# Matmul operands of odd width made even in an attention and long-convolution kernel

## The chip, the cores and the metric

The kernel runs on one core of a Trainium2 chip. The metric is device time in microseconds, the median of several executions. Before the change it is 371.0 us (three runs: 370.59, 371.0 and 372.24 us).

In the profile PE is TensorE (matmuls), PEld is TensorE loading the stationary operand, DVE is VectorE, ACT is ScalarE, POOL is GpSimd and SP is SyncE, which issues most transfers. "L905" is line 905 of the kernel. A matmul has a stationary operand (up to 128 columns, loaded ahead) and a moving operand, which is streamed through; "128\*128 128x65" is a matmul with 128 rows and 128 columns of weights and a moving operand of 65 columns.

## The reference

Softmax attention with an extra 1 in the denominator, and behind it a gated long convolution along the sequence, done by a real Fourier transform. The shapes: batch 8, 12 heads, sequence S = 448, head width 64, so the model width D is 768.

```python
scores = scale * np.matmul(q, k.transpose(0, 1, 3, 2))
m = np.max(scores, axis=-1, keepdims=True)
e = np.exp(scores - m)
attn = e / (np.sum(e, axis=-1, keepdims=True) + np.exp(-m) + 1e-09)
x = np.matmul(attn, v)                         # then [batch, S, 768]
proj = x @ w_proj                              # three parts of 768: x1, x2, x3
X2 = np.fft.rfft(x2, n=S, axis=1)
H = np.fft.rfft(filter_fft, n=S, axis=0)[None, :, :]
x2_conv = np.fft.irfft(X2 * H, n=S, axis=1)
out = (x1 * x2_conv * x3) @ w_out
```

Inputs and output are 32-bit floats; the kernel computes its matmuls in bfloat16 and sums in 32 bits.

## The kernel before

The kernel has 48 attention steps (8 batches by 6 pairs of heads, `attention(i)`) and 8 dense steps (one for each batch, `dense(b)`), woven into one another. Every piece of work is a task given to a planner by `add(...)`, with its engine, an estimate of its cost, what it needs and what it makes. The order in which the tasks are issued on each engine is written out by hand, a long list of numbers in `plan.ORDER`, one for each `add` in the order of the calls. The planner goes through it in a small model of the chip only to assign the eight banks of PSUM (each 512 columns of 32 bits); the order on an engine does not depend on the costs. So each engine runs one fixed sequence, and waits for semaphores where its next instruction needs another engine's result.

An attention step: `scores` multiplies the transposed keys kT and queries qT, 64 rows for each head of the pair (L866, moving operand of 448 columns) and one matmul of 128 rows for the last 64 keys of both heads (L868). `exps` writes the exponentials e and er to SBUF (ACT, L879 and L885). Then the exponentials are the stationary operand and the values the moving one: `out_rests` (L897) makes 4 by 2 matmuls of 64 rows for the last keys, the two heads one after the other on the upper and lower 64 rows, and `out_rest` (L905) makes 12 of 128 rows for each head. The value tiles vn hold 64 value columns and a column of ones for each head, so a matmul also gives the sum of the exponentials: their width is DH + 1 = 65 columns, and a pair of PSUM banks takes 2 heads by 4 blocks by 65 columns (`out_banks`). `norm` (DVE: L918, L919, L920) divides by that sum plus one, and frees the banks. GpSimd casts the values from 32 bits into vn (L531, L695, and L551, L649 for the last keys) and sets the ones once for each of the two vn buffers (`ones`, L1506).

A dense step for batch b: the real Fourier transform is made of four tables (pg = 0 to 3: cosine and sine, even and odd frequencies) on a folded sequence. `first` and `second` (DVE, L1045 and L1050) fold x to four parts of FQ = 113 columns. The folded tile xf is laid out as [4 parts, 6 blocks of D, 114], of which 113 columns are used, so the four parts of one block are not next to each other. In batches 0 to 2 xf is the stationary operand of the projection (`proj2`, L1073). In batches 3 to 7 it is the moving one (`still2`, L1095): four runs of 113 columns, 452 in all, written to a PSUM bank as 452 columns next to each other, six matmuls for each of six blocks, 180 in all. `still2_back` copies the bank to SBUF (DVE L1106, ACT L1108). Then come the spectrum (L1144, L1148), its product with the filter's (DVE), and the inverse transform: `inverse` (L1243) makes four matmuls for each of six blocks, 192 in all, with the inverse table bt as the moving operand, 113 columns, and writes them to 4 by 113 columns of a bank; `inverse_back` (ACT, L1252) copies these to cr. DVE unfolds cr and multiplies by the gates x1 and x3, which are projections of x as well (`gate`, L1196, 448 columns, 576 matmuls). `output` (L1009, 384 columns) is the last projection, and `project_back` (ACT, L1318) and a transfer write it out.

The table bt is made once in `more_tables` (`turn_back`, L788 and L791).

Of the kernel before, what the change touches and what calls it, by code (L numbers as in the profile page):

```python
# [15 lines left out]
BF16 = mybir.dt.bfloat16  # L16
I32 = mybir.dt.int32

B, H, S, DH = 8, 12, 448, 64
D = H * DH  # L20
SP = 112
NST = S // SP
NDT = D // 128
NHP = H // 2
SCALE = 1.0 / float(np.sqrt(DH))
DCH = 384
HALF = S // 2
FQ = SP + 1
# [286 lines left out]
def kernel(  # L315
# [11 lines left out]
    nc = tc.nc  # L327
# [6 lines left out]
    WHOLE = (5, 6, 7)  # L334
# [22 lines left out]
    const = ctx.enter_context(tc.tile_pool(name="const", bufs=1))  # L357
    wts = ctx.enter_context(tc.tile_pool(name="wts", bufs=1))
# [4 lines left out]
    fold = ctx.enter_context(tc.tile_pool(name="fold", bufs=1))  # L363
# [5 lines left out]

    ft = wts.tile([FQ, 4, FQ], BF16, name="ft")  # L370
    fr = hyp.tile([FQ, 4, FQ], BF16, name="fr", tag="yR")
    bt = wts.tile([FQ, 4, FQ], BF16, name="bt")
    wproj_bf = wts.tile([128, NDT, 3 * D], BF16, name="wproj_bf")
    wout_bf = wts.tile([128, NDT, D], BF16, name="wout_bf")

# [18 lines left out]

    kT = [const.tile([128, NHP, 4, 128], BF16, name=f"kT{i}") for i in range(2)]
    qT = [const.tile([128, NHP, S], BF16, name=f"qT{i}") for i in range(2)]
    vn = [const.tile([128, NHP, 7, DH + 1], BF16, name=f"vn{i}") for i in range(2)]
    ks_flat = const.tile([128, NHP * 128], BF16, name="ks")
    ks = ks_flat.rearrange("p (g c) -> p g c", g=NHP)

# [10 lines left out]
    x2s = nat[:, 0:KNAT].rearrange("p (t a n) -> p t a n", t=NDT, a=4)  # L411
# [33 lines left out]
    def bank(hy):  # L445
        i = plan.banks[hy][0]
        return psum[:, 512 * i : 512 * i + 512]
# [5 lines left out]
    def pair(hy):  # L453
        i = plan.banks[hy][0]
        return psum[:, 512 * i : 512 * i + 1024].rearrange("p (u n) -> p u n", u=2)
# [310 lines left out]
    def more_tables():  # L766
        bb = lambda: bank2(("hy", "bps"))[:, 0 : 4 * (FQ + 1)].rearrange("p (a b) -> p a b", a=4)

        def mirror():
            rps = bank(("hy", "rps"))  # L770
            nc.tensor.matmul(
                rps[:FQ, 0 : 4 * FQ], tab["jm"][:FQ, :], ft[:].rearrange("p a b -> p (a b)")
            )

        def mirror_back():

            rps = bank(("hy", "rps"))
            nc.vector.tensor_copy(fr[:].rearrange("p a b -> p (a b)"), rps[:FQ, 0 : 4 * FQ])
            nc.vector.tensor_scalar(
                fr[:, 1:3, :].rearrange("p a b -> p (a b)"), rps[:FQ, FQ : 3 * FQ], -1.0, None, op0=ALU.mult  # L780
            )

        def turn():
            for pg in range(4):
                nc.tensor.transpose(bb()[:FQ, pg, 0:FQ], tab["sb"][:FQ, pg, 0:FQ], ident_bf[:FQ, :FQ])

        def turn_back():
            nc.vector.tensor_scalar(  # L788
                bt[:, 0, 0:FQ], bb()[:FQ, 0, 0:FQ], tab["half"][:FQ, 0:1], None, op0=ALU.mult
            )  # L790
            nc.vector.tensor_copy(bt[:, 1:4, 0:FQ], bb()[:FQ, 1:4, 0:FQ])  # L791

        add("POOL", 1.1, WT, weights, need=["row"], make=["half"], after=WT)
        add("DVE", 0.25, FT, after=FT, emit=lambda: nc.vector.tensor_scalar(
            ft[:], tab["sb"][:FQ, :, 0:FQ], tab["half"][:FQ, 0:1], None, op0=ALU.mult), need=["sines", "half"],
            make=["ft"])
        add("PE", 0.25, 29.0, mirror, need=["ft", "half"], make=["rps"], take=[("hy", "rps")], after=29.0)
        add("DVE", 0.95, 25.0, mirror_back, need=["rps"], make=["fr"], take=[("yR", "fr")], give=[("hy", "rps")])
        add("PE", 0.25, BPS, turn, need=["ident", "sines"], make=["bps"], take=[("hy", "bps")], after=BPS)
        add("DVE", 0.45, BPS, turn_back, need=["bps", "half"], make=["bt"], give=[("hy", "bps")])  # L800

    W = {}
# [51 lines left out]
    def attention(i):  # L854
        b, hp = divmod(i, NHP)
        P = T.setdefault(i, {})
# [28 lines left out]
                nc.scalar.activation(to, of, AF.Exp, scale=SCALE)  # L885

        def out_banks():
            return pair(("op", i))[:, :, 0 : NST * (DH + 1)].rearrange("p u (n d) -> p u n d", n=NST)

        def out_bank(u):  # L890
            return out_banks()[:, u]
# [125 lines left out]
    def dense(b, calm=True):  # L1017

        L = {}
# [8 lines left out]
        def mem(name, make):  # L1028
            if (name, b) not in W:
                W[name, b] = make()  # L1030
            return W[name, b]
# [13 lines left out]
            nc.vector.tensor_tensor(t[:, 0 : ds.stop - ds.start], lo, hi, op=(ALU.add, ALU.subtract)[n])  # L1045

        def second(ds, pg):
            xf = mem("xf", lambda: fold.tile([128, 4, NDT, FQ + 1], BF16, name="xf"))
            t = L["uuww"[pg], ds.start][:, 0 : ds.stop - ds.start]
            nc.vector.tensor_tensor(  # L1050
                xf[:, pg, ds, 0:FQ],
                t[:, :, 0:FQ],
                t[:, :, HALF : HALF - FQ : -1],
                op=(ALU.add, ALU.subtract, ALU.subtract, ALU.add)[pg],
            )

# [13 lines left out]
        def proj2(pg, ch, hy):  # L1070
            L["P", pg, ch] = pps = bank(hy)
            for kt in range(NDT):
                nc.tensor.matmul(  # L1073
                    pps[:FQ, :DCH],
                    W["xf", b][:, pg, kt, 0:FQ],
                    wproj_bf[:, kt, D + ch * DCH : D + (ch + 1) * DCH],
                    start=(kt == 0),
                    stop=(kt == NDT - 1),
                )
# [10 lines left out]
            return mem("x2", lambda: hyp.tile([128, NDT, 4, 128], BF16, name="x2", tag="x2"))  # L1090

        def still2(dt, hy):
            L["P", dt] = pps = bank(hy)[:, 0 : 4 * FQ].rearrange("p (a n) -> p a n", a=4)
            for kt in range(NDT):
                nc.tensor.matmul(  # L1095
                    pps,
                    wproj_bf[:, kt, D + dt * 128 : D + (dt + 1) * 128],
                    W["xf", b][:, :, kt, 0:FQ],
                    start=(kt == 0),
                    stop=(kt == NDT - 1),  # L1100
                )

        def still2_back(dt):
            to, of = (x2s if b in WHOLE else W["xb", b])[:, dt, :, 0:FQ], L["P", dt]
            if dt % 2:
                nc.vector.tensor_copy(to, of)  # L1106
            else:
                nc.scalar.copy(to, of)  # L1108
# [128 lines left out]
        PLACE = (0, 1, 3, 2)  # L1237

        def inverse(dt, hy):
            L["I", dt] = cps = bank(hy)  # L1240
            for pg in range(4):
                K, par, rs = BLK_K[pg], pg // 2, pg % 2
                nc.tensor.matmul(  # L1243
                    cps[:, PLACE[pg] * FQ : (PLACE[pg] + 1) * FQ],
                    W["yh", b][:K, par, rs, dt * 128 : (dt + 1) * 128],
                    bt[:K, pg, :],
                )

        def inverse_back(dt):
            if ("cr", dt // 2) not in L:  # L1250
                L["cr", dt // 2] = small.tile([128, 2, 4, FQ], BF16, name="cr")
            nc.scalar.copy(  # L1252
                L["cr", dt // 2][:, dt % 2].rearrange("p a n -> p (a n)"), L["I", dt][:, 0 : 4 * FQ]
            )

        def halves(dp, n):
# [203 lines left out]
    with (  # L1460
# [42 lines left out]
        add("POOL", 0.8, 7.0, pads, make=["pads"], after=6.5)  # L1503

        def ones(i):
            nc.gpsimd.memset(vn[i][:, :, :, DH : DH + 1], 1.0)  # L1506
        for i in range(2):
            add("POOL", 0.08, (6.0, 24.0)[i], lambda i=i: ones(i), make=[("ones", i)],
                after=(6.5, 16.0)[i])
# [81 lines left out]
```

## Time and profile before

| what | value |
|---|---|
| median of the runs | 371.0 us |
| lowest and highest run | 370.59, 372.24 us |
| span of the profiled execution, first to last instruction | 369.2 us |
| mean granted TensorE clock in the span | 0.999 |
| transfers, mean rate | 185 GB/s, 68.41 MB |
| chain of work that ended last | L1009 1.4%, L1318 0.1% of the span |

The span is one execution under the profiler. That execution's own time outside its span isn't in the profile; the median of the three runs stands 1.8 us above the span.

The busy times of the engines say how full each is. A matmul's record is longer than the time until the next one starts, because matmuls overlap in the array; so what a matmul costs TensorE is read from the distance of starts, in the timeline, and not from the mean duration of its group. In a row of the timeline the first number is the start in us from the span's start, the second the time that the group spans, and "x24" how many instructions were put together. In a row of groups stand the count, then the busy time in us, the mean duration in ns, and the idle time before them with what ended it. In a row of waits stand the total in us, how often, and the longest.

### The profile page before, as it was taken

The page shows a single profiled execution, that of the slowest core. Times are in us where ns is not written, and L with a number is a line of the kernel's source. Part 1 is how long each engine was busy: PE and PEld are TensorE (multiplying, and loading weights), DVE is VectorE, ACT ScalarE, POOL GpSimd, SP SyncE. Part 2 cuts the span into 40 slices and gives each one's busy share as a digit, 9 for nine tenths or more (in the row PEclk, how much of TensorE's full clock was granted, in tenths as well). Part 3 has the DMA queues.
Part 4 walks back from the last instruction along what each step waited for, and adds up shares of the span by engine and source line. Part 5 has one row for each costly group of instructions (what it writes and reads, how often), then busy time and mean ns, then how long its engine had stood idle before and what let it go on. Part 6 is the DMA issues. An engine that isn't in the chain of part 4 may idle for free. (4 is left out here: it accounts for less than half of the span.)

```text
span 369.2 us, 9353 instructions
## 1 busy us (share of the span) xinstructions
PE 361.6 (98%) x3613; PEld 217.1 (59%) x3613; DVE 258.3 (70%) x671; ACT 263.0 (71%) x453; POOL 112.6 (30%) x247
## 2 busy tenths in 40 slices
PE   8999999999999999999999999999999999999995
PEld 6766665656664675654555555665556556555653
DVE  5569388967699648883796868773577845968570
ACT  6889686787777778687688468877778586545623
POOL 7862732344524455414125430411300000000000
PEclk9999999999999999999999999999999999999999
DMA  8999999797998999689999999799855064243125
GB/s 207 273 242 227 255 228 228 174 203 198 183 274 211 221 271 251 181 196 215 259 222 249 229 218 175 224 239 180 197 113 124 2 88 130 42 103 71 43 91 172
DMA packets 132019, 68.41 MB, mean 185 GB/s; under 512 B 88765, under 2 KB 128384, under 8 KB 131968
## 3 DMA queue, kind: packets, MB, share of 16 engines
q1 hardware_dynamic: 127248, 62.11, 74.0%
q0 software_dynamic: 4480, 5.41, 8.4%
q8 instruction: 29, 0.48, 0.6%
q10 hardware_dynamic: 240, 0.23, 0.3%
q14 instruction: 22, 0.18, 0.2%
HBM read 43.86 MB, written 11.01 MB: 149 GB/s over the span
## 5 line engine op out<-in xcount | busy, mean ns | idle before, releaser
L879 ACT ACTIVATE e<-psum 128x896 bf16<-128x896 f32 x138 | 122.2, 922 | 29.9 <-PE psum L866 27.9
L1196 PE MATMUL psum<-xT,wproj_bf 128*128 128x448 bf16 x576 | 121.2, 352 | 0.0
L1196 PEld LDWEIGHTS <-wproj_bf 128*128 128x128 bf16 x576 | 53.9, 98 | 45.6 <-issue 2.2
L1009 PE MATMUL psum<-wout_bf,yT 128*128 128x384 bf16 x288 | 53.1, 326 | 0.0
L663 POOL CAST nat<-nat 112x512 bf16<-112x512 f32 x36 | 23.7, 664 | 88.0 <-DMA nat<-in_q_dram 77.6
L905 PEld LDWEIGHTS <-e 128*128 128x128 bf16 x1104 | 40.5, 98 | 9.8 <-issue 5.8
L905 PE MATMUL psum<-vn,e 128*128 128x65 bf16 x1104 | 46.2, 194 | 0.0
L866 PE MATMUL psum<-qT,kT 64*128 64x448 bf16 x288 | 43.6, 358 | 2.1 <-DVE xb L920 1.4
L1162 DVE TENSOR_TENSOR t<-xs,hrs 113x768 bf16<-113x768 bf16 (+1 forms) x64 | 35.8, 588 | 7.2 <-ACT xs L1156 7.1
L1156 ACT CAST xs<-psum 112x384 bf16<-112x384 f32 (+1 forms) x64 | 29.2, 484 | 15.5 <-PE psum L1144 10.9
L1009 PEld LDWEIGHTS <-yT 128*128 128x128 bf16 x288 | 27.1, 98 | 18.7 <-issue 1.1
L1095 PE MATMUL psum<-xf,wproj_bf 128*128 128x452 bf16 x180 | 38.1, 356 | 0.0
L1318 ACT COPY osb<-psum 128x384 f32<-128x384 f32 x56 | 26.1, 485 | 14.6 <-PE psum L1009 9.3
L920 DVE TENSOR_TENSOR xb<-psum,den 128x512 bf16<-128x512 f32 x48 | 33.2, 691 | 1.7
L1212 DVE TENSOR_TENSOR g<-x,psum 128x448 bf16<-128x448 bf16 x42 | 25.9, 617 | 10.0 <-PE psum L1196 8.0
L885 ACT ACTIVATE er<-psum 128x448 bf16<-128x448 f32 x46 | 25.5, 554 | 8.1 <-PE psum L868 7.9
L1210 ACT CAST x<-psum 128x448 bf16<-128x448 f32 x42 | 22.4, 540 | 10.5 <-PE psum L1196 8.4
L1252 ACT CAST cr<-psum 128x452 bf16<-128x452 f32 x48 | 24.1, 551 | 6.3 <-PE psum L1243 6.3
L918 DVE TENSOR_SCALAR den<-psum 128x8 f32<-128x8 f32 x48 | 7.9, 164 | 28.3 <-PE psum L905 21.5
L695 POOL CAST vn<-nat 128x192 bf16<-128x192 f32 x58 | 23.1, 427 | 14.5 <-DMA nat<-in_v_dram 14.3
L1095 PEld LDWEIGHTS <-wproj_bf 128*128 128x128 bf16 x180 | 16.4, 96 | 17.1 <-issue 1.7
L1073 PE MATMUL psum<-wproj_bf,xf 128*113 128x384 bf16 x144 | 26.4, 327 | 0.0
(136 smaller groups left out, 484.7 us busy)
## 6 DMA issues: line engine op xcount, KB each, us to landing
nat<-in_q_dram SPq DMA_DIRECT2D x47, 224.0 KB, 4.3
out_dram<-osb SPq DMA_DIRECT2D x24, 384.0 KB, 3.8
nat<-in_k_dram SPq DMA_DIRECT2D x41, 192.0 KB, 4.6
nat<-in_v_dram SPq DMA_DIRECT2D x41, 192.0 KB, 4.4
wproj_bf<-in_moe_w_proj_dram POOLq DMA_DIRECT2D x2, 1152.0 KB, 12.3
rests<-in_k_dram SPq DMA_DIRECT2D x8, 192.0 KB, 4.8
rests<-in_v_dram SPq DMA_DIRECT2D x8, 192.0 KB, 3.9
out_dram<-osb SPq DMA_DIRECT2D x8, 192.0 KB, 3.9
```

Of the source, the lines that this page charges most:

```text
L866: nc.tensor.matmul(sc[:, u, 0:S], kT[b % 2][c, hp, t, :], qT[b % 2][c, hp, :])
L879: nc.scalar.activation(to, of, AF.Exp, scale=SCALE)
L905: nc.tensor.matmul(out_bank(u)[:, n, :], P["e"][1 + t][:, u * S + n * 128 : u * S + n * 128 + 128], vn[b % 2][:, hp, 4 * u + t, :], start= ...
L920: nc.vector.tensor_tensor(W["xb", b][:, hp].rearrange("p n (u d) -> p u n d", u=2), op[:, :, :, 0:DH], rec[:].unsqueeze(3).to_broadcast([1 ...
L1009: nc.tensor.matmul(ops[:n, :DCH], y[:, dt, 0:n], wout_bf[:, dt, ch * DCH : (ch + 1) * DCH], start=(dt == 0), stop=(dt == NDT - 1),)
L1073: nc.tensor.matmul(pps[:FQ, :DCH], W["xf", b][:, pg, kt, 0:FQ], wproj_bf[:, kt, D + ch * DCH : D + (ch + 1) * DCH], start=(kt == 0), stop= ...
L1095: nc.tensor.matmul(pps, wproj_bf[:, kt, D + dt * 128 : D + (dt + 1) * 128], W["xf", b][:, :, kt, 0:FQ], start=(kt == 0), stop=(kt == NDT - 1),
L1156: nc.scalar.copy(L["xs", par, ch][:K, pg % 2, :], L["Z", pg, ch][:K, :DCH])
L1162: nc.vector.tensor_tensor(t[:K], L["xs", par, ch][:K], h, op=ALU.mult)
L1196: nc.tensor.matmul(p[:, :S], wproj_bf[:, kt, 2 * part * D + dt * 128 : 2 * part * D + (dt + 1) * 128], xT()[:, kt, 0:S], start=(kt == 0), ...
L1212: nc.vector.tensor_tensor(g[:, dt, :], L["x1", dt], p[:, :S], op=ALU.mult)
L1318: nc.scalar.copy(L["os", st][:n, ch * DCH : (ch + 1) * DCH], L["O", st, ch][:n, :DCH])
```

## The change

Three moving operands get an even width. The value tiles vn have 66 columns for each head in place of 65; the second of the two ones columns gives a second copy of the sum, which nobody reads. The folded x is laid out as [6 blocks, 4 parts, 114], so that the four parts of a block are one run of 456 columns; the 114th column of each part is a sum or difference that nobody reads, and `second` writes it too. The inverse table bt has 114 columns for each part, the last one zero (a memset). The tiles in PSUM grow with them, and the copies out of PSUM skip the columns that were added. No task is added or taken away, and neither the order of the tasks nor their costs in the planner change.

```diff
-    bt = wts.tile([FQ, 4, FQ], BF16, name="bt")
+    bt = wts.tile([FQ, 4, FQ + 1], BF16, name="bt")
...
-    vn = [const.tile([128, NHP, 7, DH + 1], BF16, name=f"vn{i}") for i in range(2)]
+    vn = [const.tile([128, NHP, 7, DH + 2], BF16, name=f"vn{i}") for i in range(2)]
...
             nc.vector.tensor_copy(bt[:, 1:4, 0:FQ], bb()[:FQ, 1:4, 0:FQ])
+            nc.vector.memset(bt[:, :, FQ:], 0.0)
...
         def out_banks():
-            return pair(("op", i))[:, :, 0 : NST * (DH + 1)].rearrange("p u (n d) -> p u n d", n=NST)
+            return pair(("op", i))[:, :, 0 : NST * (DH + 2)].rearrange("p u (n d) -> p u n d", n=NST)
...
         def second(ds, pg):
-            xf = mem("xf", lambda: fold.tile([128, 4, NDT, FQ + 1], BF16, name="xf"))
+            xf = mem("xf", lambda: fold.tile([128, NDT, 4, FQ + 1], BF16, name="xf"))
             t = L["uuww"[pg], ds.start][:, 0 : ds.stop - ds.start]
             nc.vector.tensor_tensor(
-                xf[:, pg, ds, 0:FQ],
-                t[:, :, 0:FQ],
-                t[:, :, HALF : HALF - FQ : -1],
+                xf[:, ds, pg, :],
+                t[:, :, 0 : FQ + 1],
+                t[:, :, HALF : HALF - FQ - 1 : -1],
                 op=(ALU.add, ALU.subtract, ALU.subtract, ALU.add)[pg],
             )
...
-                    W["xf", b][:, pg, kt, 0:FQ],
+                    W["xf", b][:, kt, pg, 0:FQ],
                     wproj_bf[:, kt, D + ch * DCH : D + (ch + 1) * DCH],
...
         def still2(dt, hy):
-            L["P", dt] = pps = bank(hy)[:, 0 : 4 * FQ].rearrange("p (a n) -> p a n", a=4)
+            L["P", dt] = pps = bank(hy)[:, 0 : 4 * FQ + 4].rearrange("p (a n) -> p a n", a=4)
...
-                    W["xf", b][:, :, kt, 0:FQ],
+                    W["xf", b][:, kt],
...
         def still2_back(dt):
-            to, of = (x2s if b in WHOLE else W["xb", b])[:, dt, :, 0:FQ], L["P", dt]
+            to, of = (x2s if b in WHOLE else W["xb", b])[:, dt, :, 0:FQ], L["P", dt][:, :, 0:FQ]
...
-                    cps[:, PLACE[pg] * FQ : (PLACE[pg] + 1) * FQ],
+                    cps[:, PLACE[pg] * (FQ + 1) : (PLACE[pg] + 1) * (FQ + 1)],
                     W["yh", b][:K, par, rs, dt * 128 : (dt + 1) * 128],
                     bt[:K, pg, :],
...
             nc.scalar.copy(
-                L["cr", dt // 2][:, dt % 2].rearrange("p a n -> p (a n)"), L["I", dt][:, 0 : 4 * FQ]
+                L["cr", dt // 2][:, dt % 2], L["I", dt][:, 0 : 4 * FQ + 4].rearrange("p (a n) -> p a n", a=4)[:, :, 0:FQ]
             )
...
         def ones(i):
-            nc.gpsimd.memset(vn[i][:, :, :, DH : DH + 1], 1.0)
+            nc.gpsimd.memset(vn[i][:, :, :, DH : DH + 2], 1.0)
```

## The prediction

> **What bounds the kernel now.** I read the page's busy times first, then the waits of TensorE, then the groups by line and shape, and last the timeline, for the distance from one matmul's start to the next. The page and the waits:
>
> ```profile
> span 369.2 us, 9353 instructions
> PE 361.6 (98%) x3613; PEld 217.1 (59%) x3613; DVE 258.3 (70%) x671; ACT 263.0 (71%) x453; POOL 112.6 (30%) x247
> ...
> PEclk9999999999999999999999999999999999999999
> ...
> PE psum L866 <- DVE xb L920: 1.4, 3, 0.6
> PE psum L1487 <- DVE idle L1475: 1.1, 1, 1.1
> PE psum L866 <- DVE kT L578: 0.7, 1, 0.7
> ...
> ACT e L879 <- PE psum L866: 27.9, 37, 2.0
> DVE den L918 <- PE psum L905: 21.5, 23, 2.3
> ```
>
> TensorE is busy 98% of the span at full granted clock, and its visible waits come to 3.2 us. The two largest engines beside it wait for it (ACT 27.9 us in one group, DVE 21.5 us in another), not it for them. So the time is the sum of the matmuls' distances in TensorE's one order, and a shorter distance is worth its count. The mean durations in the groups below do not show this distance, since a matmul's record overlaps the next one's: L905 has 1104 records of 194 ns in 46.2 us. The counts are what I take from these rows:
>
> ```profile
> L1196 PE MATMUL psum<-xT,wproj_bf 128*128 128x448 bf16 x576 | 121.2, 352 | 0.0
> L905 PE MATMUL psum<-vn,e 128*128 128x65 bf16 x1104 | 46.2, 194 | 0.0
> L1095 PE MATMUL psum<-xf,wproj_bf 128*128 128x452 bf16 x180 | 38.1, 356 | 0.0
> L897 PE MATMUL psum<-vn,er 64*128 64x65 bf16 x368 | 13.5, 191 | 0.0
> L1243 PE MATMUL psum<-bt,yh 113*128 113x113 bf16 x96 | 11.9, 214 | 0.0
> L1243 PE MATMUL psum<-bt,yh 112*128 112x113 bf16 x96 | 11.8, 214 | 0.0
> L905 PE MATMUL psum<-vn,wout_bf 128*128 128x65 bf16 x48 | 1.9, 194 | 0.0
> L897 PE MATMUL psum<-vn,wout_bf 64*128 64x65 bf16 x16 | 0.6, 193 | 0.0
> ```
>
> The distances come from pairs of neighbouring groups in the timeline of TensorE: the start of the next group less the start of this one, over this one's count.
>
> ```profile
> 352.27 4.70 PE L1196 MATMUL psum<-xT,wproj_bf 128*128 128x448 bf16 x24
> 356.81 0.49 PE L1009 MATMUL psum<-wout_bf,yT 128*128 128x384 bf16 x2
> ...
> 186.32 1.14 PE L1009 MATMUL psum<-wout_bf,yT 128*128 128x384 bf16 x6
> 187.29 0.33 PE L1144 MATMUL psum<-x,ft 113*112 113x384 bf16 x1
> ...
> 22.86 0.38 PE L981 MATMUL psum<-ident_bf,xb 128*128 128x128 bf16 x4
> 23.08 0.36 PE L771 MATMUL psum<-ft,jm 113*113 113x452 bf16 x1
> ...
> 150.55 0.92 PE L905 MATMUL psum<-vn,e 128*128 128x65 bf16 x24
> 151.31 0.37 PE L1243 MATMUL psum<-bt,yh 113*128 113x113 bf16 x4
> ...
> 107.83 0.79 PE L1243 MATMUL psum<-bt,yh 113*128 113x113 bf16 x12
> 108.46 0.35 PE L1196 MATMUL psum<-xT,wproj_bf 128*128 128x448 bf16 x1
> ...
> 205.38 3.67 PE L1095 MATMUL psum<-xf,wproj_bf 128*128 128x452 bf16 x18
> 208.90 0.91 PE L905 MATMUL psum<-vn,e 128*128 128x65 bf16 x24
> ```
>
> Widths that the change leaves alone: 448 columns take 4.54/24 = 189.2 ns, 384 take 0.97/6 = 162 ns, 128 take 0.22/4 = 55 ns. They lie on one line: (189.2 - 55)/320 = 0.42 ns a column and some 2.5 ns for each matmul. Widths that it changes: 65 columns take 0.76/24 = 31.7 ns, 113 take 0.63/12 = 52.5 ns, four runs of 113 (452 in all) take 3.52/18 = 195.5 ns. The line gives 29.6, 49.6 and 190.8 ns for these. Each of the three shapes whose runs are odd lies above the line, by 2.1, 2.9 and 4.7 ns. No shape of even runs does.
>
> The Trainium skill, page "TensorE: Matmul & The Clock Gate", section "Wait — 56ns, not 53.3ns?", says that a warm matmul follows the last after N columns at 2.4 GHz plus about 2.5 ns, whatever N's parity. By it the change can only cost, for it adds columns. The trace agrees at 448 columns (189.2 ns) and contradicts it at 113 (52.5 against 49.6 ns).
>
> **The change part by part.** I take the excess to be the price of an odd run, so that the new widths fall on the line: 66 columns 30.0 ns, 114 columns 50.0 ns, 456 columns 192.5 ns.
>
> - Value tiles of 66, L905: 1104 + 48 = 1152 matmuls by 31.7 - 30.0 = 1.7 ns is 1.96 us. Bounds: 1152 by 0.4 ns more, or 0.5 us lost, if the excess stays and the column is paid on top; and 1.96 us won.
> - The same tiles in L897: 368 + 16 = 384 matmuls of 64 rows, issued as 192 pairs on the two halves of the array. The trace gives no clean distance for a pair, so between nothing and 192 by 1.7 ns = 0.33 us; I take 0.15 us, the middle.
> - Inverse tables of 114, L1243: 192 by 52.5 - 50.0 = 2.5 ns is 0.48 us. Bounds: 192 by 0.4 = 0.1 us lost to 0.48 us won.
> - Folded x as one run of 456, L1095: 180 by 195.5 - 192.5 = 3.0 ns is 0.54 us. This term needs the least: whether the excess is from odd runs or from the three breaks between runs, both are gone. Bounds: 180 by 1.7 ns = 0.3 us lost to 0.54 us won.
>
> The sum is 1.96 + 0.15 + 0.48 + 0.54 = 3.1 us of TensorE's order.
>
> The rest of the diff lies on other engines:
>
> ```profile
> L920 DVE TENSOR_TENSOR xb<-psum,den 128x512 bf16<-128x512 f32 x48 | 33.2, 691 | 1.7
> L1252 ACT CAST cr<-psum 128x452 bf16<-128x452 f32 x48 | 24.1, 551 | 6.3 <-PE psum L1243 6.3
> L1050 DVE TENSOR_TENSOR xf<-u 128x339 bf16<-128x339 bf16 x30 | 11.4, 389 | 0.1
> L1050 DVE TENSOR_TENSOR xf<-w 128x339 bf16<-128x339 bf16 x30 | 11.3, 386 | 0.3
> L1085 DVE CAST x<-psum 113x384 bf16<-113x384 f32 x12 | 6.5, 554 | 4.9 <-PE psum L1073 4.6
> L1506 POOL MEMSET vn<- 128x42 bf16 x2 | 0.5, 344 | 0.0
> L1390 DVE MEMSET low<- 128x48 f32 x1 | 0.1, 98 | 0.0
> ```
>
> The copies out of PSUM (L1252, L1106, L1108) keep their 452 elements and read them in rows of 113 at a pitch of 114. L920 already reads rows of 64 at a pitch of 65, and its 512 elements cost 691 - 554 = 137 ns over L1085's 384, or 1.07 ns an element, with nothing left for breaks. So nothing, with ACT's 551 ns hidden under TensorE as it is now. The folds (L1050) write 342 in place of 339 elements: a few ns by 64, below 0.2 us of DVE. Were the engine to take them element by element, as it does L920's, they would cost 342 by 1.07 ns and 691 - 512 by 1.07 = 143 ns, 509 ns in all, or 120 ns more by 64 = 7.7 us of DVE, a rise from 70% to 72%: still under TensorE, but up to 1 us later for the first projection of a batch, where other matmuls stand ahead of it in the order. The new memset on DVE is one of some 100 ns, in the set-up, before L1243's first use. The ones (L1506, twice) go from 42 to 84 elements: 0.3 us more each at most by their own row, on GpSimd ahead of the casts queued behind them, due at 6 and 24 us in the plan; what waits for them is the first L897 of a batch, which also needs an exponential. I count none of it. No DMA, wait or instruction order changes: the order is a fixed list, and no task is added to it.
>
> **What becomes of the 3.1 us.** Where TensorE stands still for another engine, time won since that engine's last input is lost again. The waits above are L866's for the banks that L920 frees (1.4 us in three places), and L920 itself follows L905, so even there most of the gain passes on. I let nine tenths through: 2.8 us. Made against the profiled execution this is 369.2 - 2.8 = 366.4 us of span. The median of the runs is 371.0, 1.8 us above that span, and I take these 1.8 us as fixed: **371.0 - 2.8 = 368.2 us**, 0.75% less. A difference under about 0.5% (1.9 us) is what a measurement of this kernel can't tell from none.
>
> **The rivals.**
>
> - *The weight load is the limit at 65 columns.* L905 loads 128 new columns of weights for each matmul of only 65, and no row here has a shorter matmul that would show how fast loads can follow each other. If 31.7 ns is the load's pace, a 66th column changes nothing there and L897 and L905 give nothing. Left are 0.48 + 0.54 = 1.0 us, by nine tenths 0.9: 370.1 us. For it: L905's excess, 2.1 ns, is smaller than the other two. Against it: L1243, whose 52.5 ns leave more room for the load, has an excess as well. Chance 0.2.
> - *The grain is coarser than two.* All widths on the line (448, 384, 128) are multiples of 16. If the moving operand is taken in eights or sixteens, 65 and 66 cost the same, as do 113 and 114; 65 as 72 columns would be 32.5 ns and 113 as 120 would be 52.5 ns by the line, close to what the rows show. Then only the 456 gain: 0.54 by nine tenths is 0.5 us, 370.5 us. Against it: four runs of 113 taken as 4 by 120 would be 202.5 ns, and the row has 195.5. Chance 0.16.
> - *Columns cost and parity is free: slower.* If the excess belongs to short or narrow matmuls as such, each added column is paid at 0.42 ns: 0.5 us in L905, 0.08 in L1243, 0.08 in L897's pairs and 0.3 in L1095, 0.95 us in all, which TensorE, with no slack, passes on whole: 371.9 us. It decides as soon as 66 columns take over 31.7 ns. For it: the line's slope holds in every row. Against it: L1095 is neither short nor narrow and has the largest excess. Chance 0.06. The page named above gives the same time, and the trace already departs from it at all three shapes.
>
> **How the numbers follow.** Forecast 0.58, weight load 0.2, coarser grain 0.16, columns cost 0.06. The forecast's own range is 367.3 (all 3.1 us pass, and 0.6 us of scatter, for the runs of before lie from 370.59 to 372.24) to 369.4 (half of L905's term missing, nine tenths of the rest, and 0.3 us of scatter). The next two cases lie at 370.1 and 370.5, so the range is drawn from 367.3 to 371.0, which takes them in with half a microsecond of scatter and leaves out the slower case and the tails. Faster by over 0.5% (below 369.1): most of the forecast's 0.58, and scatter, 0.56. Slower by over 0.5% (above 372.9): only if the added columns cost and something in the folds is late too, 0.04. Within: 0.40.
>
> **What the changed kernel's profile would show.** In the timeline, L905's distance at 30.0 ns in groups of 24 (31.7 or more: the weight load, or the grain); L1243's at 50.0 (52.5: the grain); L1095's at 192.5; L1196's unchanged at 189.2. The page should have TensorE still at 98% and a span near 366.4. L1050 should stay near 390 ns and L1252 near 551. The prediction is wrong if the distances fall but the span doesn't: then TensorE's waits in the waits view must have grown by as much, L866's for L920 first, or a wait for a DMA stands there, of which the view of before has none.

## The result, and the profile after

| | before | after |
|---|---|---|
| median of the runs | 370.95 us (6 runs, 370.59 to 372.24) | 369.02 us (6 runs, 368.5 to 370.53) |
| span of the profiled execution | 369.2 us | 366.7 us |

The ratio is 0.9951, with a 95% interval from 0.9932 to 0.9969: the kernel gained 1.8 us, between 1.2 and 2.5. A second comparison, with 12 and 29 runs, gave 0.9964 (0.9945 to 0.9983), or 1.3 us. The forecast was 368.2 us; the time came out 0.8 us above it.

The page of the changed kernel, its top and the TensorE clock. The lines of the code behind the new memset have moved by one, so L905 is L906 here, L1095 is L1096, and so on:

```profile
span 366.7 us, 9354 instructions
...
PE 358.6 (98%) x3613; PEld 215.5 (59%) x3613; DVE 258.3 (70%) x672; ACT 262.8 (72%) x453; POOL 112.5 (31%) x247
...
PEclk9999999999999999999999999999999999999999
```

Its waits of TensorE (total, times, longest):

```profile
PE psum L867 <- DVE xb L921: 1.4, 3, 0.6
...
PE psum L867 <- DVE kT L578: 0.8, 1, 0.8
```

TensorE is as full as it was, it waits for the same things about as long as it did, and its busy time fell by 3.0 us (361.6 to 358.6). So far this looks like the forecast. The groups by line and shape say otherwise (count, then busy time in us, which changes as the sum of the matmuls' distances does, then the mean of one in ns):

```profile
L906 PE MATMUL psum<-vn,e 128*128 128x66 bf16 x1104 | 45.9, 194 | 0.0
...
L1096 PE MATMUL psum<-xf,wproj_bf 128*128 128x456 bf16 x180 | 37.6, 357 | 0.0
L921 DVE TENSOR_TENSOR xb<-psum,den 128x512 bf16<-128x512 f32 x48 | 33.2, 691 | 1.7
...
L1253 ACT CAST cr<-psum 128x452 bf16<-128x452 f32 x48 | 24.1, 552 | 6.2 <-PE psum L1244 6.2
...
L898 PE MATMUL psum<-vn,er 64*128 64x66 bf16 x368 | 13.4, 191 | 0.0
...
L1244 PE MATMUL psum<-bt,yh 113*128 113x114 bf16 x96 | 11.9, 214 | 0.0
L1244 PE MATMUL psum<-bt,yh 112*128 112x114 bf16 x96 | 11.8, 214 | 0.0
...
L1051 DVE TENSOR_TENSOR xf<-w 128x342 bf16<-128x342 bf16 x30 | 11.4, 389 | 0.3
L1051 DVE TENSOR_TENSOR xf<-u 128x342 bf16<-128x342 bf16 x30 | 11.0, 374 | 0.1
...
L906 PE MATMUL psum<-vn,wout_bf 128*128 128x66 bf16 x48 | 1.8, 194 | 0.0
...
L1507 POOL MEMSET vn<- 128x84 bf16 x2 | 0.3, 175 | 0.0
L792 DVE MEMSET bt<- 113x4 bf16 x1 | 0.1, 62 | 0.0
```

The value matmuls went from 46.2 + 1.9 to 45.9 + 1.8 us, the folded x from 38.1 to 37.6, L897's from 13.5 to 13.4, the inverse not at all. That is 1.0 us in the four terms, where the forecast had 3.1. The timeline confirms it for the two long groups: the next group starts 3.47 us after L1096's 18 matmuls began, 192.8 ns each, as forecast (192.5), and 0.63 us after L1244's 12, 52.5 ns each, as before:

```profile
203.36 3.63 PE L1096 MATMUL psum<-xf,wproj_bf 128*128 128x456 bf16 x18
206.83 0.92 PE L906 MATMUL psum<-vn,e 128*128 128x66 bf16 x24
...
106.00 0.79 PE L1244 MATMUL psum<-bt,yh 113*128 113x114 bf16 x12
106.63 1.30 PE L1197 MATMUL psum<-xT,wproj_bf 128*128 128x448 bf16 x6
```

**Where the other 1.5 us of the profiled pair come from.** The start. Three rows of TensorE's timeline before, the same three after, and then those of another execution of the kernel before (the control e2 below): the first scores, the first idle matmuls among the work, and the first value matmuls.

```profile
6.67 1.30 PE L866 MATMUL psum<-qT,kT 64*128 64x448 bf16 x6 [0.66 <-DVE kT L578]
...
9.61 1.48 PE L1479 MATMUL psum<-idle 128*128 128x128 bf16 x19
...
14.43 0.93 PE L905 MATMUL psum<-vn,e 128*128 128x65 bf16 x24
```

```profile
5.99 0.74 PE L867 MATMUL psum<-qT,kT 64*128 64x448 bf16 x6 [0.81 <-DVE kT L578]
...
8.22 1.22 PE L1480 MATMUL psum<-idle 128*128 128x128 bf16 x19
...
12.79 0.93 PE L906 MATMUL psum<-vn,e 128*128 128x66 bf16 x24
```

```profile
6.67 0.74 PE L866 MATMUL psum<-qT,kT 64*128 64x448 bf16 x6 [0.66 <-DVE kT L578]
...
8.66 1.22 PE L1479 MATMUL psum<-idle 128*128 128x128 bf16 x19
...
13.41 0.93 PE L905 MATMUL psum<-vn,e 128*128 128x65 bf16 x24
```

The first value matmuls start at 14.43 us before and at 12.79 after, 1.64 us earlier, though no width has mattered yet. In the first execution L866's six matmuls span 1.30 us, in the other two 0.74: TensorE ran at about half speed until 10.1 us there, until 4.1 us in the profile of after and until 6.0 us in the control. In all three the 128-column matmuls before that time stand 107 ns apart and those after it 56 ns, and the traces' first record of the clock, at full speed, starts at 10.1, 4.1 and 6.0 us. The control is the same kernel as the first and starts its value matmuls 1.0 us sooner. So of the 1.64 us only some 0.6 are left for the change, and single profiles can't say whether even these are its own.

For the comparisons below I divide every span in three: the **start** (up to the first L905, a row of the timeline), the **standstills** after it (each distance of neighbouring matmuls is compared with the smallest at the same place of TensorE's order in any trace of the table further below, and what exceeds it by more than 40 ns is summed), and the **rest**, which is the matmuls' own pace.

### The profile page after: what moved, and what is told of

It is laid out like the page before. It is cut to its first block, busy times and chain, and to the rows that moved or that the text cites. A ratio compares the mean times of both kernels' runs of the same rounds, so it can differ in the third digit from the quotient of the medians.

```text
span 366.7 us, 9354 instructions
## 1 busy us (share of the span) xinstructions
PE 358.6 (98%) x3613; PEld 215.5 (59%) x3613; DVE 258.3 (70%) x672; ACT 262.8 (72%) x453; POOL 112.5 (31%) x247
## 3 DMA queue, kind: packets, MB, share of 16 engines
q1 hardware_dynamic: 127248, 62.11, 72.3%
## 5 line engine op out<-in xcount | busy, mean ns | idle before, releaser
L906 PEld LDWEIGHTS <-e 128*128 128x128 bf16 x1104 | 40.2, 97 | 9.8 <-issue 5.6
L906 PE MATMUL psum<-vn,e 128*128 128x66 bf16 x1104 | 45.9, 194 | 0.0
L1163 DVE TENSOR_TENSOR t<-xs,hrs 113x768 bf16<-113x768 bf16 (+1 forms) x64 | 35.0, 575 | 7.0 <-ACT xs L1157 6.6
L1096 PE MATMUL psum<-xf,wproj_bf 128*128 128x456 bf16 x180 | 37.6, 357 | 0.0
L1096 PEld LDWEIGHTS <-wproj_bf 128*128 128x128 bf16 x180 | 16.7, 98 | 16.4 <-issue 1.7
L695 POOL CAST vn<-nat 128x192 bf16<-128x192 f32 x58 | 22.2, 411 | 13.0 <-DMA nat<-in_v_dram 12.8
```

Source lines behind the costliest of these rows:

```text
L906: nc.tensor.matmul(out_bank(u)[:, n, :], P["e"][1 + t][:, u * S + n * 128 : u * S + n * 128 + 128], vn[b % 2][:, hp, 4 * u + t, :], start= ...
L1096: nc.tensor.matmul(pps, wproj_bf[:, kt, D + dt * 128 : D + (dt + 1) * 128], W["xf", b][:, kt], start=(kt == 0), stop=(kt == NDT - 1),)
L1163: nc.vector.tensor_tensor(t[:K], L["xs", par, ch][:K], h, op=ALU.mult)
```

## The experiments

**e1_after and e2_before: both kernels again, for a firm interval and two more profiles.**

> The changed kernel again. Theory 'even width' (the recorded forecast): 2.5 us or more below the kernel before in every round, whatever the start does. Theory 'grain of eight and a lucky start': the steady part gains only 0.9 us, and the rest of the measured gain is TensorE's clock coming up at 4 us in place of 10 us, by chance of the execution; then runs fall in two groups about 1.7 us apart, near 368.6 and 370.2 us, and the kernel before shows the same two groups near 369.4 and 371.0 us, in shares of their own.

> The kernel before again, as a control with a trace of its own. Theory 'lucky start': its clock comes up at about 4 us or about 10 us, as it falls out, and runs near 369.4 us are among its rounds. Theory 'the change brings the clock up sooner': all runs near 371.0 us and the first 128-column matmuls 107 ns apart until about 10 us.

e1: 369.14 us, ratio 0.9964 (0.9945 to 0.9983). e2: 370.57 us, 0.9996 (0.9979 to 1.0012). The gain is real, and the ruler is good to about 0.2% either way. The rest is 354.24 and 354.22 us in the two profiles of before, and 353.40 and 353.38 in the two of after: 0.84 us less, repeatable to 0.02.

**e3_xf_only: the folded x as one run of 456 columns, nothing else.**

```diff
-            xf = mem("xf", lambda: fold.tile([128, 4, NDT, FQ + 1], BF16, name="xf"))
+            xf = mem("xf", lambda: fold.tile([128, NDT, 4, FQ + 1], BF16, name="xf"))
...
-                    W["xf", b][:, :, kt, 0:FQ],
+                    W["xf", b][:, kt],
```

> Only the folded x as one run of 456 columns; value and inverse tables stay odd. All theories: L1095 at 192.5 ns for 195.5, 0.5 us over 180 matmuls. 'Even width': that is a sixth of the gain. 'Grain of eight': more than half of the steady gain (0.5 of 0.9 us). So 370.5 us if the start falls as in most runs of before, 1.7 us less if the clock comes up early.

370.38 us, 0.9981 (0.9965 to 0.9998). Its group of the profile, with 38.1 us before:

```profile
L1095 PE MATMUL psum<-xf,wproj_bf 128*128 128x456 bf16 x180 | 37.6, 356 | 0.0
```

The distance is 192.8 ns, the rest 353.80 us, 0.43 us less than before. This term is close to what the forecast said it was (2.7 ns a matmul in place of 3.0).

**e5_value_tile_only: the value tiles at 66 alone. e6_tile_66_matmul_65: the tile has rows of 66, but the matmul still streams 65. e10_one_column_of_ones: as e6, with one column of ones, as before.** The forecast took the 66th column itself as the cure; e6 leaves it out and keeps the new spacing.

```diff
-    vn = [const.tile([128, NHP, 7, DH + 1], BF16, name=f"vn{i}") for i in range(2)]
+    vn = [const.tile([128, NHP, 7, DH + 2], BF16, name=f"vn{i}") for i in range(2)]
...
-                        vn[b % 2][:, hp, 4 * u + t, :],
+                        vn[b % 2][:, hp, 4 * u + t, 0 : DH + 1],
```

> Only the value tiles at 66 columns; xf and bt as before. By the traces so far 1536 matmuls of 66 columns save 0.45 us in place of 2.1. 'Even width, rest is the start': 370.4 us, 0.45 us below before. 'The ones are on the early path': the memset of the ones on GpSimd takes 175 ns in place of 344, twice in a row ahead of a key cast that TensorE waits for near 11 us, and more comes through: 370.0 us or less. Together with xf alone (0.45 us) it should give the whole change's 1.7 us if nothing else plays a part.

> Value tiles of 66 columns with both columns set to one, but matmuls that stream 65 of them, in PSUM as before: the memory layout without the matmul width. 'The ones are on the early path': about 0.35 us below before (370.5 us), the GpSimd memset at 175 ns, L905's distance as before. 'Width alone': no difference (370.8 us). If rows of 66 columns (132 bytes, each value row on a word boundary) are what speeds L905 up, its distance falls to 31.5 ns here too.

> Value tiles 66 columns apart, 65 streamed, and only one column set to one, as before: against e6 it takes the second column of ones away. 'The GpSimd memset': it takes 344 ns again in place of 175, and e6's gain falls by 0.35 us, to 370.1 us; 'the row's start': 0.45 us from L905 at 31.5 ns stays in any case. If the time is that of e6 (369.75 us), the memset is worth nothing and e6's gain beyond 0.45 us is from elsewhere.

The two groups of e6, to be set beside 46.2 and 1.9 us before, and 45.9 and 1.8 after:

```profile
L905 PE MATMUL psum<-vn,e 128*128 128x65 bf16 x1104 | 45.8, 193 | 0.0
...
L905 PE MATMUL psum<-vn,wout_bf 128*128 128x65 bf16 x48 | 1.8, 193 | 0.0
```

The matmul is 65 columns wide as before, and the whole gain of L905 is there. Averaged over 1082 gaps the distance is 31.92 ns before, 31.53 in e5, e6 and e10, 31.55 after. So it isn't the odd width that is paid for, but that the rows of the tile lie 65 elements apart. The times: e5 369.33 us, 0.9952 (0.9933 to 0.9970); e6 369.75, 0.9961 (0.9945 to 0.9976); e10 369.81, 0.9969 (0.9953 to 0.9986). The rest falls by 0.41 to 0.46 us in all three. But e6 as measured gained 1.4 us (0.9 to 2.0): about 1 us of it is in no matmul distance. The memset of the ones doesn't explain it: e10 has the old one, and agrees with e6 within the intervals.

**e4_widths, e8_widths_as_used, e11_starts: widths and places measured by themselves.** In place of the 38 idle matmuls at the kernel's start stand groups of 24 (12 for the long ones) of each kind; their results are read by nobody, and the times of these kernels mean nothing. In e4 each group reads its moving operand at one fixed place:

```diff
-            for _ in range(SPIN):
+            for _ in range(110):
+                nc.tensor.matmul(t[:, 0:128], idle, idle)
+            for n in WIDTHS:
+                for _ in range(24):
+                    nc.tensor.matmul(t[:, 0:n], idle, wide[:, 0:n])
```

> The kernel before, with its 38 warm-up matmuls replaced by 24 matmuls at each of many widths of the moving operand, on a tile of zeros (its time means nothing, only distances do). 'Even width': 66 at 30.0 and 114 at 50.0 ns, 65 and 113 some 2 to 3 ns above. 'Grain of eight': distances step at 65, 73, 81, 113, 121 and are flat between, 64 at 29.2, 65 to 72 at one value, 113 to 120 at one value near 52.5 ns; 112 at 49.2 ns. 'Weight load is the limit': all widths from 32 to about 70 at the same 31.5 ns, and 112 to 116 on the line. One run of 65 that starts at an odd element as against an even one: no theory expects a difference. Four runs of 113 at 195.5, four runs of 112 at 189.2.

From the trace, start to start, mean of the group in ns:

```
columns   32    48    56    64*   65    66    68    72   80    96   112   113   114   116   120   121   122   128
ns      25.2  25.0  25.8  29.0  30.4  30.4  31.1  32.5  35.7  42.5  49.2  50.0  50.0  50.8  52.5  53.3  53.3  55.8
columns  448    450    452    456    457   4x112  4x113  4x114  (runs 224 apart)
ns     189.2  190.0  190.8  192.5  193.3   189.2  192.7  192.7
* median; a pause of about 1 us fell into this group
```

Three readings. 113 costs what 114 costs, 65 what 66 does, 121 what 122 does, and four runs of 113 what four of 114 do: in every pair measured **an odd width costs as much as the next even one, no more**. Short matmuls go down to 25 ns, each behind a weight load of 128 columns (the trace has one load for each of them), so the load doesn't limit at 65. And 113 columns stand 50.0 ns apart here, but 52.5 in the kernel: what makes the 2.5 ns is something else than the width.

e8 adds what differs in the kernel, one thing at a time: 113 rows, the place in PSUM, the start of the moving operand, the weights.

```diff
+            for i in range(24):
+                o = 113 * (i % 4)
+                nc.tensor.matmul(t[:, 0:113], idle, wide[:, o : o + 113])
```

> Matmuls of 113, 114, 112, 65, 66, 64, 72 and 452 or 456 columns one after the other in the warm-up, each with one thing of the kernel's use added: 113 rows, four places in PSUM, four places of the moving operand, other weights each time, then all together; only distances count. On a tile of one place 113 and 114 took 50.0 ns, in the kernel they take 52.5. 'It is the operand's place': the row with moving places, or with places in PSUM, at 52.5, the others 50.0. 'It is the weights': the row with other weights at 52.5. 'It is other engines' traffic': all rows at 50.0, also with everything together. For 452 columns at the kernel's pitch of 684: 195.5 if the pitch or the start of rows is the cause, else 192.5.

The timeline of e8. L1494 is 113 columns at one place, L1496 with 113 rows, L1499 with four places in PSUM, L1502 with the start at 113 times 0 to 3, L1505 with other weights each time; L1517 is 65 columns at one place with other weights each time, L1520 the same with the start at 65 times 0 to 2 and four places in PSUM; L1508, L1511 and L1514 have all of it, at 113, 114 and 112 columns and spacing; L1533, L1536 and L1539 are four runs of 113, four of 114 and one of 456:

```profile
11.95 1.36 PE L1494 MATMUL psum<-kT,idle 128*128 128x113 bf16 x24
13.15 1.36 PE L1496 MATMUL psum<-kT,idle 113*128 113x113 bf16 x24
14.35 1.36 PE L1499 MATMUL psum<-kT,idle 128*128 128x113 bf16 x24
15.55 1.41 PE L1502 MATMUL psum<-kT,idle 128*128 128x113 bf16 x24
16.80 1.36 PE L1505 MATMUL psum<-kT 128*128 128x113 bf16 x24
18.00 1.41 PE L1508 MATMUL psum<-kT 113*128 113x113 bf16 x24
19.24 1.40 PE L1511 MATMUL psum<-kT 113*128 113x114 bf16 x24
20.48 1.34 PE L1514 MATMUL psum<-kT 113*128 113x112 bf16 x24
21.66 0.89 PE L1517 MATMUL psum<-kT 128*128 128x65 bf16 x24
22.39 0.92 PE L1520 MATMUL psum<-kT 128*128 128x65 bf16 x24
...
25.38 2.51 PE L1533 MATMUL psum<-kT,idle 128*128 128x452 bf16 x12
27.72 2.50 PE L1536 MATMUL psum<-kT,idle 128*128 128x456 bf16 x12
30.06 2.47 PE L1539 MATMUL psum<-kT,idle 128*128 128x456 bf16 x12
32.37 1.50 PE L1541 MATMUL psum<-idle 128*128 128x128 bf16 x24
```

One place: 1.20/24 = 50.0 ns, and as much with 113 rows and with other places in PSUM. Changing start: 1.25/24 = 52.1 ns. Other weights: 1.20/24 = 50.0 ns, and 65 columns take 0.73/24 = 30.4 ns with them, as in e4. All together: 51.7 ns at 113 and at 114, 49.2 at 112. Four runs take 2.34/12 = 195.0 ns with 113 as with 114 columns, one run of 456 takes 192.5. So the excess belongs to starts that change (for the folded x all of it, for the inverse a part: it stands 52.9 ns apart in the kernel and 51.7 here). 113 and 114 both change them, which is why the inverse gained nothing; 112 is a multiple of 8 elements, or 16 bytes, and pays nothing.

e11 asks whether a single odd start is at fault or the change from one to the next. Its kind of edit, for rows 65 and 72 apart:

```diff
+            for i in range(24):
+                nc.tensor.matmul(t[:, 0:65], idle, wide[:, 65 * (i % 6) : 65 * (i % 6) + 65])
...
+            for i in range(24):
+                nc.tensor.matmul(t[:, 0:65], idle, wide[:, 72 * (i % 6) : 72 * (i % 6) + 65])
```

> Matmuls of 113, 65 and other widths, 24 at a time, whose moving operand starts 0, 1, 2, 4, 8, 16 and 24 columns (0 to 48 bytes) into a tile; then 65 columns from rows 65, 66, 68, 72 and 80 apart; only distances count. 'Start of the moving row': 113 at 50.0 ns from a start at 0, 8, 16 or 24 columns and 52.5 from 1, 2 and 4; if eight bytes are enough, 50.0 from 4 as well. 65 columns: 30.3 from rows 72 or 80 apart, 31.5 or more from 65 and 66. 'Width': no start matters.

The timeline of e11: 65 columns from rows 65, 66, 68, 72 and 80 elements apart.

```profile
31.59 0.94 PE L1534 MATMUL psum<-kT,idle 128*128 128x65 bf16 x24
32.36 0.92 PE L1536 MATMUL psum<-kT,idle 128*128 128x65 bf16 x24
33.12 0.91 PE L1538 MATMUL psum<-kT,idle 128*128 128x65 bf16 x24
33.87 0.89 PE L1540 MATMUL psum<-kT,idle 128*128 128x65 bf16 x24
34.59 0.89 PE L1542 MATMUL psum<-kT,idle 128*128 128x65 bf16 x24
35.32 2.44 PE L1544 MATMUL psum<-kT,idle 128*128 128x448 bf16 x12
```

The rows resolve 0.4 ns a matmul; averaged over the single starts of the trace the distances are 32.2, 31.5, 31.1, 30.4 and 30.4 ns. With one fixed start for all 24, 113 columns take 50.0 ns from element 0, 2, 4, 8, 16 or 24, and 50.8 from element 1. A fixed start is free, but for that 0.8 ns; a start whose place within 16 bytes differs from the last one's costs, and less the more even the spacing.

**e9_rows_on_16_bytes: after, with the value rows 72 and the inverse table's rows 120 elements apart; still 66 and 114 columns are streamed.** By e11 this should win what 66 and 114 leave. (The room comes from small set-up tiles that now share one tile, or lie in the place of the output weights until those are loaded; their load waits for that.)

```diff
-    bt = wts.tile([FQ, 4, FQ + 1], BF16, name="bt")
+    bt = wts.tile([FQ, 4, 120], BF16, name="bt")
...
-    vn = [const.tile([128, NHP, 7, DH + 2], BF16, name=f"vn{i}") for i in range(2)]
+    vn = [const.tile([128, NHP, 7, 72], BF16, name=f"vn{i}") for i in range(2)]
```

> The changed kernel with every moving row started at a multiple of 16 bytes: value tiles 72 columns apart (144 bytes, 66 streamed), inverse tables 120 apart (240 bytes, 114 streamed); the folded x is so already (912 bytes). To find room, the idle tile and one table lie in the place of the output weights, and small scalars share a tile. Theory 'start of the moving row': L906 falls from 31.5 to 30.3 ns (1152 by 1.2 = 1.4 us), L1244 from 52.5 to 50.0 (0.5 us), and the time by 1.9 us below the changed kernel's 369.1: 367.2 us. Theory 'width': nothing more than the changed kernel, 369.1 us.

369.47 us, 0.9945 (0.9927 to 0.9963), which can't be told from after, where 367.2 us was expected. Its groups:

```profile
L907 PE MATMUL psum<-vn,e 128*128 128x66 bf16 x1104 | 45.0, 193 | 0.0
...
L1245 PE MATMUL psum<-bt,yh 113*128 113x114 bf16 x96 | 11.7, 213 | 0.0
L1245 PE MATMUL psum<-bt,yh 112*128 112x114 bf16 x96 | 11.7, 213 | 0.0
```

The matmuls did what e11 said: 45.9 to 45.0 us and 23.7 to 23.4, and the rest is 352.35 us, 1.04 us below after's and 1.87 below before's. But its profile has 2.28 us of standstills where after has 0.54. Something else was lost with the move; since set-up tiles moved and a load waits as well, this run alone doesn't say what.

**e7_early_fillers: after, with ten more idle matmuls before 8 us,** to bring TensorE's clock up sooner, should the start be where the gain comes from.

```diff
-    FILL = (8.0, 44.0, 0.9)
+    FILL = (4.0, 44.0, 0.9)
```

> The changed kernel with up to ten idle matmuls more in TensorE's first gaps, before 8 us, so that its clock comes up sooner. 'The start is part of the spread': its runs lie closer together than those of the changed kernel (368.5 to 372.0 us), median up to 0.5 us lower, 368.7 us. If the clock is not what spreads the runs: 369.1 us as before, or up to 0.5 us more for what the idle matmuls delay.

369.9 us, 0.9956 (0.9940 to 0.9972): no better than after. In its profile TensorE came up at 6.9 us, within the scatter of the others (3.9 to 10.3 us).

**e12_pad_on_before: the missing microsecond.** What e5, e6, e10, after and e1 have in common, and e2, e3 and e9 don't, is not a matmul. Section 3 of the profile's page gives the share of 16 transfer engines that the first queue's 127248 packets took; times the span, times 16, over the packets, this is the mean time of a packet. It is 34.4 ns in before, 34.8 in e2, 34.5 in e3 and 34.6 in e9, but 33.3 in after, 32.6 in e1, 32.1 in e5, 32.6 in e6, 32.7 in e10 and 33.9 in e7. (e4, e8 and e11, whose tiles lie as in before, have 34.6, 34.9 and 33.9, so at 33.9 the two groups meet.) The value tiles grew from 5460 to 5544 bytes a partition, and all that is allocated behind the two of them moved by 192 bytes; among that are the rooms where the loads of queries, keys and values land (in e9 they moved by 1152), and also the weights, the gates, the spectra and the output's buffers. e12 is the kernel before, with an unused tile of 192 bytes behind the value tiles:

```diff
     vn = [const.tile([128, NHP, 7, DH + 1], BF16, name=f"vn{i}") for i in range(2)]
+    pad = const.tile([128, 96], BF16, name="pad")
```

> The kernel before with one unused tile of 192 bytes a partition put behind the value tiles, so that every tile allocated after them (the rooms in which the loads land among them) starts 192 bytes further on, at the same places as in the changed kernel; all matmuls and their operands are those of before. Theory 'the places of the loads': the value tiles' greater size is what makes the transfers' packets shorter, and these give the part of the gain that the matmuls' distances do not show. Then the 1024-byte packets take some 56 ns here as well, the first queue is busy some 260 to 269 us in place of 273 to 276, and the time is 1.0 us below before, some 0.997 of it, with L905 still 31.9 ns apart. Rival 'the rows of the value tile': the packets stay at some 60 ns, the queue at 273 us or more, and the time is that of before within 0.3 us (0.999 to 1.001). If the packets get shorter and the time stays, the packets explain nothing of the time.

369.93 us, 0.9971 (0.9956 to 0.9986): **1.1 us (0.5 to 1.6) from a tile that nobody touches.** The first queue (packets, MB, share of 16 engines), of before and then of e12:

```profile
q1 hardware_dynamic: 127248, 62.11, 74.0%
```

```profile
q1 hardware_dynamic: 127248, 62.11, 71.0%
```

74.0% of 369.2 us is 273 us of queue time, 71.0% of 367.9 is 261. The same bytes in the same packets take 4% less time. By size the packets part without an overlap: the 10528 of 1024 bytes, by their bytes the loads of q, take 58.0 to 61.3 ns on average in the seven traces without this 192-byte move (before, e2, e3, e4, e8, e9, e11) and 54.3 to 56.4 ns in the seven with it; the 3584 of 3072 bytes, by their bytes the output, take 137 to 142 and 136 to 142 ns, no different. The matmuls are untouched, as the three parts of the spans show:

| kernel | value rows apart | first queue's mean packet, ns | start | standstills | rest | ratio |
|---|---|---|---|---|---|---|
| before | 65 | 34.4 | 14.43 | 0.54 | 354.24 | 1 |
| e2, before again | 65 | 34.8 | 13.41 | 0.84 | 354.22 | 0.9996 |
| e12, pad alone | 65 | 32.8 | 13.22 | 0.46 | 354.20 | 0.9971 |
| e3, xf alone | 65 | 34.5 | 13.73 | 1.57 | 353.80 | 0.9981 |
| e5, value tile alone | 66 | 32.1 | 12.76 | 1.16 | 353.81 | 0.9952 |
| e6, 65 of 66 | 66 | 32.6 | 13.55 | 0.64 | 353.80 | 0.9961 |
| e10, e6 with old ones | 66 | 32.7 | 14.52 | 1.30 | 353.78 | 0.9969 |
| after | 66 | 33.3 | 12.79 | 0.54 | 353.40 | 0.9951 |
| e1, after again | 66 | 32.6 | 13.14 | 0.41 | 353.38 | 0.9964 |
| e9, rows of 72 and 120 | 72 | 34.6 | 13.18 | 2.28 | 352.35 | 0.9945 |

The rest obeys the layouts to 0.02 us: 0.4 for the value rows, 0.4 for the folded x, 0.84 for both, nothing for the pad, nothing for the inverse. What each measured gain holds beyond the rest is 1.0 us in e12, 1.4 in e5, 1.0 in e6, 0.7 in e10, 1.0 in after and 0.5 in e1, all with the move, and 0.1 in e2, 0.3 in e3 and 0.2 in e9, all without; each of these is uncertain by some 0.6 us. Late transfers should show as standstills. The waits of TensorE in e3, and those in e9, have a row that no profile with the 192-byte move has:

```profile
PE psum L866 <- DMA kT<-nat: 0.7, 1, 0.7
```

```profile
PE psum L870 <- DMA kT<-nat: 0.6, 1, 0.6
```

e2 has the same row, with 0.5 us, but before's own profile hasn't, and e10 stands still for 1.30 us with the move. One profiled execution of each kernel is too little to split the pad's microsecond between start and standstills; e12 against e2 shows 0.2 us of the one and 0.4 of the other. Shown is that the places of the tiles behind the pad change the time, and with it the packets of the loads. That the time is won by way of the packets is argued and not shown, and which tile it is, and which boundary it has to keep, is open. In the built programs the large landing room begins at 68928 bytes in before, at 69120 in after and e12 (a multiple of 512) and at 70080 in e9, which fits a boundary of 512 bytes and was not tested further.

## Why the prediction was right, and where it wasn't

Its sign and its range held, for reasons that are half its own: of 3.1 us of distance 0.84 came true, and about as much again came from a move of tiles that it had counted as nothing. That the time fell within 0.8 us of the forecast is luck.

- **TensorE's pace is the time.** Right, as far as it can be seen. The 0.84 us of distance is not lost again to waits: the standstills are 0.54 and 0.84 us in the profiles of before and 0.54 and 0.41 in those of after. The nine tenths were too careful.
- **The line.** The prediction took 0.42 ns a column and 2.5 ns for each matmul from its rows, but through 189.2 and 55 ns the constant would be 1.3 ns; the row of four 128-column matmuls is too short to give it. e4 puts it right, with 55.8 ns at 128 columns and 189.2 at 448: the line as used holds.
- **L1095, 0.54 us.** Right: 0.43 us by the rest of e3, 0.5 by the groups. The reading behind it was open between odd runs and breaks. Breaks as such cost nothing (four runs of 112 take 189.2 ns in e4, as 448 in one run do). Four runs of 113 cost what four of 114 do (192.7 ns), and changing starts add the rest, up to 195.5.
- **L905, 1.96 us: the step that failed.** The prediction took the whole excess over the line (31.7 against 29.6 ns) as the price of an odd run. But at a fixed start 65 columns cost what 66 do, 30.4 ns in e4, and what stands above that belongs to the changing start. A spacing of 66 removes 0.4 ns of that, not 1.7: 0.4 us. A spacing of 72 removes 1.1.
- **L1243, 0.48 us.** Failed for the same reason: 114 columns, 114 apart, change the start just as 113 do. No row that the prediction showed had an even width with starts that change within 16 bytes; such a row alone would have told the two readings apart.
- **L897, 0.15 us.** 0.1 us by the groups, at the edge of what they resolve.
- **What was left out: 1.1 us.** The prediction said "No DMA, wait or instruction order changes". No transfer was added, but the tiles behind the values moved by 192 bytes, the loads' rooms among them, and e12 gives that move alone 1.1 us (0.5 to 1.6), more than any term of the sum turned out to be worth. It makes up for about half of the 2 us that L905 and L1243 failed to give.
- **The other engines.** Right: L1252 went from 551 to 552 ns, L920 stayed at 691, the folds are no slower (389 and 374 ns with 342 elements). The memset of bt takes 62 ns. The ones cost less with twice the elements (344 to 175 ns each), not more.
- **The rivals.** The weight load as the limit falls by e4 (25 ns at 32 to 56 columns). The coarser grain falls as well (116, 118 and 120 columns have their own prices, 0.8 ns apart), though it had named the right losers, L905 and L1243. That columns cost and parity is free holds in part: two columns cost 0.8 ns, but the odd ones were paid already.

The Trainium skill, page "TensorE: Matmul & The Clock Gate", section "Wait — 56ns, not 53.3ns?", says N columns at 2.4 GHz plus about 2.5 ns. At one fixed place e4 agrees with it at every even width from 112 up (50.0 ns at 114, 55.8 at 128, 192.5 at 456). At 113 columns it gives 49.6 ns, where e4 measured 50.0 and e8 52.1 with changing starts; the measurement decides. By it alone this change would have cost time.

## What to carry to other kernels

In what was measured here, a moving operand is cheapest when the distance from one matmul's start to the next, and from one run to the next within a matmul, is a multiple of 16 bytes (rows of 72 and 80 elements, or 112); the width may then be odd, and pays for one column more. An excess over a line tells that something is paid for, not what: before pricing a cure, look for a row, or make one, that has the suspected property without its neighbour (here an even width with changing starts). And a tile that grows moves every tile behind it: a gain of a few tenths of a per cent from a layout is not the layout's until a pad of the same size has been tried alone. Rows of 72 and 120 together with the loads' places of after were not tried; by the table they should give about 1.9 + 1.1 = 3 us against before, an estimate.

## What the runs showed of the hardware that wasn't expected

- An odd width of the moving operand costs what the next even one does: 113 and 114 columns 50.0 ns, 65 and 66 columns 30.4 ns.
- Starts that change within 16 bytes cost 1 to 2 ns a matmul: 113 columns 52.1 ns in place of 50.0, 65 columns 32.2 ns with rows 65 apart and 30.4 with rows 72 apart. In the kernel itself rows of 120 brought L1243 only from 52.9 to 51.7 ns; what keeps it from 50.0 is open.
- 192 bytes of displacement in SBUF changed the first queue's mean packet time from 34.4 ns to 32.8, that of its 1024-byte packets from 59.9 to 55.7, and the kernel's time by 0.3%.
- TensorE's 128-column matmuls stand 107 ns apart at first, and this ends between 3.9 and 10.3 us after the span's start, in executions of like kernels. The clock row of the page shows full speed throughout (9 in each slice, mean 0.999); the trace's record of the clock begins only at that time, so before it the distances are the only witness.
- A GpSimd memset of 42 single elements of 2 bytes takes 344 ns, one of 84 in pairs takes 175.
